# Reordering the first head pair and moving two PSUM uses in a fused hash-attention and adapter kernel

## The chip, the cores and the metric

The kernel runs on one core of a Trainium2 chip. Five engines work side by side, each through its own list of instructions: TensorE (PE, matrix products and transposes), VectorE (DVE), ScalarE (ACT), GpSimd (POOL) and SyncE (SP, here only the issue of DMAs). They meet at semaphores. The metric is the device time of one execution in microseconds (us), the median of several runs; lower is better.

## The reference

The first half is attention in which a query sees only the keys of its own hash bucket; the second sends each row of the result, heads side by side, through two of eight low-rank adapters.

```python
# q, k, v: (B, H, S, D) = (4, 8, 768, 64) float32; proj: (64, 6)
q_bucket = sum over 6 bits of (q @ proj > 0) * 2**bit      # k_bucket likewise
mask   = q_bucket[:, :, :, None] == k_bucket[:, :, None, :]
scores = where(mask, q @ k.T / sqrt(D), -1e9)
attn   = exp(scores - max) / (sum + 1e-9)
x      = (attn @ v), heads side by side                    # (3072, 512)
logits = x @ w_gate                                        # 8 experts
w      = softmax over the top 2 of logits
out    = x + sum over the 2 experts e of w_e * (x @ A[e]) @ B[e]   # A: 512x16, B: 16x512
```

## The kernel before

**Tiling.** The 32 heads are taken as 16 pairs (`p` = 0 to 15), four pairs to a batch. A pair has 2 x 768 x 768 scores, transposed (keys on partitions, queries along the row): nine tiles of 128x1024 (`s` = 0 to 8). For each, `score(p, s)` issues the matmuls (line 323) and one exponential on ScalarE (line 325) from PSUM to the bf16 tile `P`. The mask costs no pass of its own: the bf16 operand `aug[p % 2]` has 71 rows, 64 of q or k, six of signs (plus or minus 0.5, one per hash bit) and one constant, so that a score of two different buckets is pushed below what the exponential can hold. The uniform term (`uniform`, line 359: a matmul of a tiny constant with the sum of v, then a copy on VectorE) gives rows without a partner their mean.

**One pair's preparation.** `trans(p, g)`, g = 0, 1, 2, turns four 128x128 blocks of q and k at a time on TensorE (line 238) and evicts them to `qkT` (VectorE, line 245, or ScalarE). `cast` (POOL, line 276) writes 64 rows of `aug`. `hash(p)` multiplies `qkT` by the six projections (four matmuls, line 258), thresholds them to signs on VectorE (`sgn`, line 261), and SP moves the signs into `aug` by small DMAs (`sign_dma`, line 164), two in `hash`, two in `hash_b`. `vcast` (POOL) turns v to bf16 and sums it. `pvmm(p, h, i0, i1)` multiplies P by v for row blocks i0 to i1 - 1 of head h, six matmuls each (line 330); `norm` divides by the sums on VectorE (lines 374 to 379) and casts to bf16 on POOL (385).

**The adapters.** `xturn` (a transposing DMA) or, for the last pair of a batch, `xtrans` (six PE transposes into `xtp`, line 458, and a copy to `xT` on VectorE, line 460) turn x. The row blocks ("slots") of the batch before are then worked off by `moe_slot` beside the attention of later pairs: `lgz` (gate and A product, line 475), `route` (top two), `zmtrans` (line 529), `delta` (line 543). `moe_group(p)` gives two slots to pairs 5, 6, 9 and 10, one to 7, 8, 11 and 12, three to 13 and 14, and none to pairs 0 to 4.

**What sets the order.** The order is written out by hand (`tc.manual_schedule()`): `run` calls `score(p, s)`, then `first_pair(s)` for pair 0 or `pair(p, s)` for pairs 1 to 14, and `moe_slot(p, s)`; `last_pair` writes out pair 15. Every engine does its part in that order. So does SP's queue: a DMA that must wait for data holds up all DMAs that SP issues after it. PSUM has four pools: `ps_s` with two buffers of 128x1024 (score tiles), `ps_t` with one bank ("t"), `ps_v` with two ("v", the results of `pvmm`) and `ps_m` with one ("m"). A use of a bank waits until the use before it in the program has been read out.

**The first pair.** In `prologue` head 0 of pair 0 gets its own short way: `turn0` transposes it, `signs0` (line 134) computes its signs with `pst`, straight into `aug` by one threshold on VectorE for the queries and one for the keys (line 142). Head 1's signs come from `hash0(1, ...)` behind score tile 0 of pair 0: two matmuls into `hsf` (line 151) with the packed projection `proj2` (copied on VectorE, line 101), the threshold `sgnf` (line 154) and two DMAs from SP. Half of score tile 4, the first that reaches head 1, waits for those DMAs. In `first_pair` the loads of q and k of pair 2 are issued ahead of `hash0`, those of v of pairs 1 and 2 behind it:

```python
        if s == 0:
            self.load_qk(2)
            self.hash0(1, (self.nc.sync, self.nc.sync))
            self.load_v(1)
            self.load_v(2)
        if s < 3:
            self.trans(1, s, bank=None if s == 1 else (self.ps_m, "m"))
```

Of the kernel before, what the change touches and what calls it, by code (L numbers as in the profile page):

```python
# [12 lines left out]
F32 = mybir.dt.float32  # L13
# [6 lines left out]
class Emitter:  # L20
# [46 lines left out]
    def prologue(self):  # L67
        nc, sg, P, T, D, S = self.nc, self.singles, self.P, self.T, self.D, self.S

        self.pst = sg.tile([P, 6], F32, name="pst")  # L70
        nc.scalar.dma_start(out=self.pst, in_=self.proj.unsqueeze(0).to_broadcast([2, D, 6]))
        nat = self.natp.tile([P, 2, 2, T * D], F32, tag="nat", name="nat0")
        self.nat[0] = nat
        for h in range(2):
            for i, src in enumerate((self.q, self.k)):
                nc.sync.dma_start(out=nat[:, i, h], in_=src[0, h].rearrange("(p t) d -> p (t d)", t=T))
        self.load_qk(1)
        self.load_v(0)

        self.eps = sg.tile([P, P], BF16, name="eps")  # L80
        nc.vector.memset(self.eps, 2.0 ** -56)
        self.ident = sg.tile([P, P], F32, name="ident")
        make_identity(nc, self.ident)
        first = sg.tile([P, 1], F32, name="first")
        nc.scalar.activation(out=first, in_=self.eps[:, 0:1], func=ACT.Exp)
        self.proj2 = sg.tile([P, 32], F32, name="proj2")
        nc.vector.memset(self.proj2, 0.0)

        self.aug = [sg.tile([P, 4, S], BF16, name=f"aug{i}") for i in range(2)]
        for j in range(8):  # L90
            eng = nc.vector if j < 2 else nc.gpsimd
            eng.memset(self.aug[j // 4][64:96, j % 4, :], (1.0, -1.5)[j % 2])
        self.qkT[0] = self.qktp.tile([P, 2 * S], F32, tag="qkT", name="qkT0")
        self.warm(19)
        self.turn0(0, self.ps_s, "s")
        self.half0(0, 0, nc.scalar.copy)
        self.half0(0, 1, nc.scalar.copy)
        self.signs0()
        self.turn0(1, self.ps_v, "v")
        for e in range(2):  # L100
            nc.vector.tensor_copy(out=self.proj2[64 * e:64 * e + 64, e:12:2],
                                  in_=self.pst[64 * e:64 * e + 64, :])
        self.half0(1, 0, nc.gpsimd.tensor_copy)
        self.half0(1, 1, nc.gpsimd.tensor_copy)

        self.vb = []
        for i in range(3):
            a = sg.tile([P, 2, T + 1, D + 1], BF16, name=f"vb{i}")
            nc.gpsimd.memset(a[:, :, 0:T, D:D + 1], 1.0)
            nc.gpsimd.memset(a[:, :, T:T + 1, D:D + 1], float(T))  # L110
            self.vb.append(a)
        self.vcast(0)
        self.ident_bf = sg.tile([P, P], BF16, name="ident_bf")
        nc.gpsimd.tensor_copy(out=self.ident_bf, in_=self.ident)
        self.wa = sg.tile([P, self.nD, self.LZ], BF16, name="wa")
        self.Bcat = sg.tile([self.ER, self.Dm], BF16, name="Bcat")
        self.warm(6)
# [14 lines left out]


    def signs0(self):
        nc, P = self.nc, self.P
        for i in range(2):
            hs = self.ps_s.tile([P, 2, 512], F32, tag="s", name=f"hsd{i}")
            for e in range(2):
                nc.tensor.matmul(out=hs[64:70, e, 0:384], lhsT=self.pst[64 * e:64 * e + 64, :],
                                 rhs=self.qkT[0][64 * e:64 * e + 64, i * 384:(i + 1) * 384],  # L140
                                 start=True, stop=True)
            nc.vector.tensor_scalar(out=self.aug[0][64:70, i, :].rearrange("p (e c) -> p e c", e=2),
                                    in0=hs[64:70, :, 0:384], scalar1=0.0, scalar2=0.5,
                                    op0=ALU.is_gt, op1=ALU.subtract)

    def hash0(self, h, engs):
        nc = self.nc
        hs = self.ps_t.tile([self.P, 384], F32, tag="t", name=f"hsf{h}")
        rows = slice(64 * h, 64 * h + 64)
        for i in (2 * h, 2 * h + 1):  # L150
            nc.tensor.matmul(out=hs[32 * i:32 * i + 32, :], lhsT=self.proj2,
                             rhs=self.qkT[0][:, i * 384:(i + 1) * 384], start=True, stop=True)
        sgn = self.sgp.tile([self.P, 384], BF16, tag="sgn", name=f"sgnf{h}")
        nc.vector.tensor_scalar(out=sgn[rows], in0=hs[rows], scalar1=0.0, scalar2=0.5,
                                op0=ALU.is_gt, op1=ALU.subtract)
        for i in range(2):
            self.sign_dma(engs[i], 0, 2 * h + i, sgn)

    def half0(self, h, e, copy):
        copy(out=self.aug[0][0:64, 2 * h:2 * h + 2, e * 384:(e + 1) * 384],  # L160
# [190 lines left out]
        return p >= self.n_pairs - self.PPB  # L351


    def uniform(self, p):
        if self.uni_pe(p):
            return
        n = self.D + 1
        ps = self.ps_t.tile([self.P, 2, n], F32, tag="t", name=f"un{p}")
        self.nc.tensor.matmul(out=ps, lhsT=self.eps, rhs=self.vb[p % 3][:, :, self.T, :], start=True, stop=True)  # L359
        self.uni[p] = self.smallp.tile([self.P, 2, n], F32, tag="uni", name=f"uni{p}")  # L360
        self.nc.vector.tensor_copy(out=self.uni[p], in_=ps)  # L361
# [171 lines left out]
        self.acc[b, slots] = self.accp.tile([P, 3, self.Dm], F32, tag="acc", name=f"acc{b}_{slots[0]}")  # L533


    def delta(self, b, slots, i, by_pool=False, eng=None, parts=1):
        nc, P, S = self.nc, self.P, self.S
        acc, last = self.acc[b, slots], b == self.B - 1
        rows = self.out[b * S:(b + 1) * S, :].rearrange("(p t) f -> p t f", t=self.T)
        n = self.Dm // parts  # L540
        ps = (self.ps_s if last else self.ps_m).tile(
            [P, self.Dm], F32, tag="s" if last else "m", name=f"dl{b}_{slots[i]}")
        nc.tensor.matmul(out=ps, lhsT=self.zmT[b, slots][:, i * P:(i + 1) * P], rhs=self.Bcat,  # L543
                         start=True, stop=True)
        for c in [slice(j * n, (j + 1) * n) for j in range(parts)]:
            if by_pool:
                tmp = self.xp.tile([P, self.Dm], F32, tag="tmp", name=f"tmp{b}_{slots[i]}")
                nc.scalar.activation(out=tmp, in_=ps, func=ACT.Copy, scale=self.rt[b, slots][:, i:i + 1])  # L548
                nc.gpsimd.tensor_add(out=acc[:, i, :], in0=tmp, in1=self.x[b][:, slots[i], :])  # L549
            else:  # L550
                nc.vector.scalar_tensor_tensor(out=acc[:, i, c], in0=ps[:, c], scalar=self.rt[b, slots][:, i:i + 1],  # L551
                                               in1=self.x[b][:, slots[i], c], op0=ALU.mult, op1=ALU.add)
            if last:
                (eng or nc.sync).dma_start(out=rows[:, slots[i], c], in_=acc[:, i, c])
        if not last and i == len(slots) - 1:
            nc.sync.dma_start(out=rows[:, slots[0]:slots[0] + len(slots), :], in_=acc[:, 0:len(slots), :])
# [42 lines left out]
        self.last_pair(N - 1, self.B - 1)  # L599

    def first_pair(self, s):
        if s == 0:
            self.load_qk(2)
            self.hash0(1, (self.nc.sync, self.nc.sync))
            self.load_v(1)
            self.load_v(2)
        if s < 3:
            self.trans(1, s, bank=None if s == 1 else (self.ps_m, "m"))
        if s == 3:
            self.cast(1, 0)  # L610
            self.cast(1, 1)
        if s == 4:
            self.hash(1)
            self.hash_b(1)
            self.uniform(0)
        if s == 5:
            self.vcast(1)
            self.load(3)
        if s == 6:
# [1 line left out]
            self.trans(2, 0)  # L621
        if s == 7:
            self.pvmm(0, 0, 2, 4)
            self.trans(2, 1, bank=(self.ps_m, "m"))
        if s == 8:
            self.pvmm(0, 0, 4, 6)
            self.load_moe(0)
            self.load_moe(1)

    def pair(self, p, s):  # L630
        if s == 0:
            self.norm(p - 1, 0)
            self.trans(p + 1, 2)
            self.load_qk(p + 3, (0,))
        if s == 1:
            self.pvmm(p - 1, 1, 0, 2)
            self.cast(p + 1, 0)
            self.cast(p + 1, 1)
        if s == 2:
# [1 line left out]
            if p + 1 == self.n_pairs - 1:  # L641
                self.hash_b(p + 1)
            self.load_qk(p + 3, (1,))
        if s == 3:
            self.pvmm(p - 1, 1, 2, 4)
        if s == 4:
            self.pvmm(p - 1, 1, 4, 6)
            self.uniform(p)
            if p + 1 < self.n_pairs - 1:
                self.hash_b(p + 1)  # L650
        if s == 5:
            self.norm(p - 1, 1)
            self.vcast(p + 1)
            self.trans(p + 2, 0, on_act=len(self.moe_group(p)[1]) > 1)
            if p < 4:
                self.load_moe(p + 1)
            if p == 3:
# [8 lines left out]
        if s == 8:  # L666
            self.pvmm(p, 0, 3, 6)
            if p % self.PPB == 0:
                self.xtrans(p - 1)
            self.load_v(p + 3)  # L670

    def last_pair(self, p, b):
# [102 lines left out]
```

## Time and profile before

| | |
|---|---|
| median of five runs | 176.09 us |
| the five runs | 175.36, 175.99, 178.79, 176.09, 177.24 us |
| the profiled execution | 175.36 us |
| its span (first to last instruction) | 173.6 us |
| TensorE clock granted, mean | 0.984 of full speed |
| TensorE busy | 161.1 us, 93% of the span |
| ScalarE busy | 150.8 us, 87% |
| VectorE busy | 116.1 us, 67% |
| POOL busy | 115.5 us, 67% |
| the 144 exponentials, mean of one | 1029 ns |
| first score tile of pair 0 on TensorE | 7.65 us after the start of the span |
| first score tile of pair 1 | 18.75 us |

Lines of the profile name the line of the kernel, the engine, the operation, what it writes and reads (`P<-s`: the tile P from s), the shape and the count. "Idle before" is the time for which the engine had stood still just before, with the event that ended it. The chain of work that ended last is followed back from the last instruction, at each step to what released it; it shows which engine held up the end at which time. Loads of q, k and v are 384 KB each, a transfer of signs 9 KB.

### The profile page before, as it was taken

How to read it: one execution, taken by the hardware profiler on the slowest of the kernel's cores; microseconds unless marked ns; L12 is line 12 of the kernel's file. 1: busy time of each engine (PE TensorE's matmuls, PEld its weight loads, DVE VectorE, ACT ScalarE, POOL GpSimd, SP SyncE). 2: the span in 40 equal slices, each digit the busy share in tenths (PEclk: the TensorE clock that was granted, in tenths of full speed). 3: DMA queues.
4: the chain of work that ended last, by engine and by line, in shares of the span. 5: the costliest groups of instructions: out<-in, count | busy, mean ns of one | idle time of the engine just before them, and what ended most of it. 6: DMA issues, size and time to landing. Idle time of an engine off the chain costs nothing.

```text
span 173.6 us, 5249 instructions
## 1 busy us (share of the span) xinstructions
PE 161.1 (93%) x2100; PEld 111.9 (64%) x2105; DVE 116.1 (67%) x312; ACT 150.8 (87%) x176; POOL 115.5 (67%) x140
## 2 busy tenths in 40 slices
PE   7888999999999999999999999999999999998850
PEld 6355667676766676767677676767676676687610
DVE  3762666565656787878687786868785676647870
ACT  3776999999998899999997999999997988997760
POOL 8399969696988667576755676676766466630280
PEclk9999999999999999999999999999999999999985
DMA  5955497879998067697877179686954024250036
GB/s 146 301 198 185 156 254 154 162 149 190 148 220 252 27 130 225 192 187 262 137 231 228 46 136 312 131 248 196 196 169 152 9 49 183 44 197 4 2 126 237
DMA packets 30438, 28.51 MB, mean 164 GB/s; under 512 B 15078, under 2 KB 28494, under 8 KB 30414
## 3 DMA queue, kind: packets, MB, share of 16 engines
q1 hardware_dynamic: 25020, 27.38, 57.3%
q0 software_dynamic: 4832, 0.27, 4.6%
q10 hardware_dynamic: 562, 0.53, 0.9%
q8 instruction: 16, 0.26, 0.6%
q14 instruction: 8, 0.07, 0.1%
HBM read 19.42 MB, written 6.29 MB: 148 GB/s over the span
## 4 chain that ended last, share of the span: by engine, by line
PE 81%; DVE 7%; POOL 3%; issue 3%; DMA 1%; ACT 1%; SPq 1%; DVEq 0%; POOLq 0%; ACTq 0%
PE s L323 33%; PE pv L330 18%; PE tr L238 12%; PE hs L258 7%; PE lz L475 4%; PE dl L543 2%; PE warm L184 1%; PE xtp L458 1%; DVE xT L460 1%; DMA aug<-sgnf 1%; POOL xb L385 1%; POOL aug L160 1%; PE ztp L529 1%; DVE acc L551 1%; DVE qkT L131 1%
## 5 line engine op out<-in xcount | busy, mean ns | idle before, releaser
L325 ACT ACTIVATE P<-s 128x1024 bf16<-128x1024 f32 x144 | 139.7, 1029 | 11.3 <-PE s L323 9.5
L323 PE MATMUL s<-aug 71*128 71x256 bf16 (+2 forms) x408 | 86.2, 316 | 1.3 <-ACT P L325 0.6
L276 POOL CAST aug<-qkT 64x1536 bf16<-64x1536 f32 x30 | 43.9, 1463 | 12.7 <-DVE qkT L245 10.1
L330 PEld LDWEIGHTS <-P 128*128 128x128 bf16 x1080 | 44.9, 98 | 11.3
L330 PE MATMUL pv<-vb,P 128*128 128x65 bf16 x1080 | 47.5, 193 | 0.2
L323 PEld LDWEIGHTS <-aug 71*128 71x128 bf16 x408 | 32.8, 97 | 19.2 <-issue 9.9
L245 DVE TENSOR_SCALAR qkT<-tr 128x512 f32<-128x512 f32 x40 | 27.4, 685 | 8.8 <-PE tr L238 8.3
L385 POOL CAST xb<-x 128x768 bf16<-128x768 f32 x15 | 12.4, 824 | 26.2 <-DVE x L379 23.9
L238 PE MATMUL tr<-ident,nat 128*128 128x128 f32 x180 | 28.3, 279 | 0.6 <-DVE xT L460 0.6
L238 PEld LDWEIGHTS tr<-ident,nat 128*128 128x128 f32 x180 | 20.2, 140 | 10.0 <-DVE qkT L245 3.1
L261 DVE TENSOR_SCALAR sgn<-hs 128x384 bf16<-128x384 f32 x15 | 8.4, 558 | 14.5 <-PE hs L258 13.0
L379 DVE TENSOR_TENSOR x<-pv,ri 128x384 f32<-128x384 f32 x30 | 16.7, 557 | 1.0
L551 DVE SCALAR_TENSOR_TENSOR acc<-dl,rt,x 128x512 f32<-128x512 f32 (+1 forms) x21 | 15.0, 719 | 3.1 <-PE dl L543 3.1
L221 POOL TENSOR_TENSOR vs<-vn 128x384 f32<-128x384 f32 x16 | 15.9, 996 | 0.0
L374 DVE TENSOR_TENSOR pv<-pv,uni 128x390 f32<-128x390 f32 x24 | 13.6, 567 | 2.5 <-PE pv L330 2.4
L219 POOL CAST vb<-vn 128x768 bf16<-128x768 f32 x16 | 13.2, 827 | 0.3 <-DMA vn<-in_v_dram 0.2
L258 PE MATMUL hs<-qkT,proj 128*32 128x384 f32 x120 | 12.8, 498 | 0.0
L549 POOL TENSOR_TENSOR acc<-tmp,x 128x512 f32<-128x512 f32 x4 | 5.0, 1263 | 8.8 <-ACT tmp L548 8.8
L475 PE MATMUL lz<-wa,xT 128*128 128x136 bf16 x96 | 9.3, 223 | 0.6 <-ACT xT L460 0.6
L543 PE MATMUL dl<-Bcat,zmT 128*128 128x512 bf16 x19 | 7.4, 391 | 1.1 <-ACT zmT L532 0.8
L361 DVE COPY uni<-un 128x130 f32<-128x130 f32 x12 | 3.5, 294 | 7.1 <-PE un L359 7.1
L224 POOL TENSOR_TENSOR vb<-vs,vs 128x128 bf16<-128x128 f32 x16 | 7.3, 457 | 1.3
(73 smaller groups left out, 121.0 us busy)
## 6 DMA issues: line engine op xcount, KB each, us to landing
vn<-in_v_dram SPq DMA_DIRECT2D x16, 384.0 KB
nat<-in_q_dram SPq DMA_DIRECT2D x15, 384.0 KB
nat<-in_k_dram SPq DMA_DIRECT2D x15, 384.0 KB
out_dram<-acc SPq DMA_DIRECT2D x4, 512.0 KB
out_dram<-acc SPq DMA_DIRECT2D x8, 256.0 KB
out_dram<-acc SPq DMA_DIRECT2D x2, 768.0 KB
aug<-sgn SPq DMA_DIRECT2D x60, 9.0 KB
nat<-in_q_dram SPq DMA_DIRECT2D x2, 192.0 KB
```

The lines of the kernel that those rows point to most:

```text
L221: nc.gpsimd.tensor_add(out=s3, in0=vn[:, :, 0:3, :], in1=vn[:, :, 3:6, :])
L238: nc.tensor.transpose(out=ps[:, j * P:(j + 1) * P], in_=self.nat[p][:, idx % 2, idx // 2, u * P:(u + 1) * P], identity=self.ident)
L245: nc.vector.tensor_scalar(out=out, in0=ps, scalar1=2.0 ** -5, scalar2=None, op0=ALU.mult)
L258: nc.tensor.matmul(out=ps[32 * j:32 * j + 32, :], lhsT=self.proj2, rhs=self.qkT[p][:, j * 384:(j + 1) * 384], start=True, stop=True)
L276: self.nc.gpsimd.tensor_copy(out=self.aug[p % 2][0:64, :, e * n:(e + 1) * n], in_=self.qkT[p][64 * e:64 * e + 64, :].rearrange("p (j c) -> ...
L323: nc.tensor.matmul(out=ps[:, o:o + n], lhsT=aug[0:71, 2 * h + 1, kt * P:(kt + 1) * P], rhs=q, start=True, stop=True)
L325: nc.scalar.activation(out=self.P_[p][:, s * 1024:(s + 1) * 1024], in_=ps, func=ACT.Exp, scale=128.0)
L330: self.nc.tensor.matmul(out=pv, lhsT=self.p_at(p, h, kt, i), rhs=self.vb[p % 3][:, h, self.slot(kt), :], start=(start and kt == 0), stop=( ...
L379: nc.vector.tensor_tensor(out=self.x[b][:, :, c:c + D].rearrange("p (u e) d -> p e u d", e=2), in0=pv[:, 0:T, 0:D].rearrange("p (e u) d -> ...
L385: nc.gpsimd.tensor_copy(out=self.xb[b][:, hp], in_=self.x[b][:, :, hp * P:(hp + 1) * P])
L475: nc.tensor.matmul(out=lz[:, i, :], lhsT=self.xT[b][:, t, s * P:(s + 1) * P], rhs=self.wa[:, t, :], start=(t == 0), stop=(t == self.nD - 1))
L551: nc.vector.scalar_tensor_tensor(out=acc[:, i, c], in0=ps[:, c], scalar=self.rt[b, slots][:, i:i + 1], in1=self.x[b][:, slots[i], c], op0= ...
```

## The change

The edits, by place:

- Prologue: the two copies into `proj2` stand ahead of the sign thresholds of head 0. The threshold for the keys becomes two instructions of 6x384 instead of one of 6x768; `signs0` is divided into helpers (`hash0`, `sign0`), and the old `hash0` becomes `hash1(p, h)` with the same instructions.
- Pair 0, SP's queue: the two sign transfers of head 1 are issued ahead of the loads of q and k of pair 2, with v of pairs 1 and 2 behind those.
- Pair 0, TensorE: the three transpose groups of pair 1 stand behind score tiles 1, 2 and 3 instead of 0, 1 and 2. They keep their banks.
- Pair 0: the uniform term stands behind tile 5 instead of tile 4, and in bank m instead of bank t.
- Pairs 5, 6, 9 and 10: `pvmm` of head 1 of the pair before takes row blocks 0; 1, 2; 3, 4; 5 behind tiles 1, 3, 4 and 5, instead of 0, 1; 2, 3; 4, 5 behind tiles 1, 3 and 4. Other pairs keep theirs.
- Pairs 4, 8 and 12, tile 8: `xtrans` of the pair before uses bank m instead of bank t.
- `delta` takes a bank as an argument, which no caller gives.

```diff
@@ -95,11 +95,11 @@
         self.turn0(0, self.ps_s, "s")
         self.half0(0, 0, nc.scalar.copy)
         self.half0(0, 1, nc.scalar.copy)
-        self.signs0()
-        self.turn0(1, self.ps_v, "v")
         for e in range(2):
             nc.vector.tensor_copy(out=self.proj2[64 * e:64 * e + 64, e:12:2],
                                   in_=self.pst[64 * e:64 * e + 64, :])
+        self.signs0()
+        self.turn0(1, self.ps_v, "v")
         self.half0(1, 0, nc.gpsimd.tensor_copy)
         self.half0(1, 1, nc.gpsimd.tensor_copy)
 
@@ -132,29 +132,39 @@
 
 
     def signs0(self):
-        nc, P = self.nc, self.P
         for i in range(2):
-            hs = self.ps_s.tile([P, 2, 512], F32, tag="s", name=f"hsd{i}")
+            hs = self.ps_s.tile([self.P, 2, 512], F32, tag="s", name=f"hsd{i}")
             for e in range(2):
-                nc.tensor.matmul(out=hs[64:70, e, 0:384], lhsT=self.pst[64 * e:64 * e + 64, :],
-                                 rhs=self.qkT[0][64 * e:64 * e + 64, i * 384:(i + 1) * 384],
-                                 start=True, stop=True)
-            nc.vector.tensor_scalar(out=self.aug[0][64:70, i, :].rearrange("p (e c) -> p e c", e=2),
-                                    in0=hs[64:70, :, 0:384], scalar1=0.0, scalar2=0.5,
-                                    op0=ALU.is_gt, op1=ALU.subtract)
-
-    def hash0(self, h, engs):
+                self.hash0(i, e, hs[:, e, 0:384])
+            if i == 0:
+                self.sign0(i, hs[:, :, 0:384], 0, 2)
+            else:
+                for e in range(2):
+                    self.sign0(i, hs[:, e:e + 1, 0:384], e, e + 1)
+
+    def hash0(self, j, e, out):
+        self.nc.tensor.matmul(out=out[64:70], lhsT=self.pst[64 * e:64 * e + 64, :],
+                              rhs=self.qkT[0][64 * e:64 * e + 64, j * 384:(j + 1) * 384],
+                              start=True, stop=True)
+
+    def sign0(self, j, hs, e0, e1):
+        self.nc.vector.tensor_scalar(
+            out=self.aug[0][64:70, j, e0 * 384:e1 * 384].rearrange("p (e c) -> p e c", c=384),
+            in0=hs[64:70], scalar1=0.0, scalar2=0.5, op0=ALU.is_gt, op1=ALU.subtract)
+
+
+    def hash1(self, p, h):
         nc = self.nc
-        hs = self.ps_t.tile([self.P, 384], F32, tag="t", name=f"hsf{h}")
+        hs = self.ps_t.tile([self.P, 384], F32, tag="t", name=f"hsf{p}_{h}")
         rows = slice(64 * h, 64 * h + 64)
-        for i in (2 * h, 2 * h + 1):
-            nc.tensor.matmul(out=hs[32 * i:32 * i + 32, :], lhsT=self.proj2,
-                             rhs=self.qkT[0][:, i * 384:(i + 1) * 384], start=True, stop=True)
-        sgn = self.sgp.tile([self.P, 384], BF16, tag="sgn", name=f"sgnf{h}")
+        for j in (2 * h, 2 * h + 1):
+            nc.tensor.matmul(out=hs[32 * j:32 * j + 32, :], lhsT=self.proj2,
+                             rhs=self.qkT[p][:, j * 384:(j + 1) * 384], start=True, stop=True)
+        sgn = self.sgp.tile([self.P, 384], BF16, tag="sgn", name=f"sgnf{p}_{h}")
         nc.vector.tensor_scalar(out=sgn[rows], in0=hs[rows], scalar1=0.0, scalar2=0.5,
                                 op0=ALU.is_gt, op1=ALU.subtract)
-        for i in range(2):
-            self.sign_dma(engs[i], 0, 2 * h + i, sgn)
+        for j in (2 * h, 2 * h + 1):
+            self.sign_dma(nc.sync, p, j, sgn)
 
     def half0(self, h, e, copy):
         copy(out=self.aug[0][0:64, 2 * h:2 * h + 2, e * 384:(e + 1) * 384],
@@ -351,11 +361,12 @@
         return p >= self.n_pairs - self.PPB
 
 
-    def uniform(self, p):
+    def uniform(self, p, bank=None):
         if self.uni_pe(p):
             return
         n = self.D + 1
-        ps = self.ps_t.tile([self.P, 2, n], F32, tag="t", name=f"un{p}")
+        pool, tag = bank or (self.ps_t, "t")
+        ps = pool.tile([self.P, 2, n], F32, tag=tag, name=f"un{p}")
         self.nc.tensor.matmul(out=ps, lhsT=self.eps, rhs=self.vb[p % 3][:, :, self.T, :], start=True, stop=True)
         self.uni[p] = self.smallp.tile([self.P, 2, n], F32, tag="uni", name=f"uni{p}")
         self.nc.vector.tensor_copy(out=self.uni[p], in_=ps)
@@ -533,13 +544,13 @@
         self.acc[b, slots] = self.accp.tile([P, 3, self.Dm], F32, tag="acc", name=f"acc{b}_{slots[0]}")
 
 
-    def delta(self, b, slots, i, by_pool=False, eng=None, parts=1):
+    def delta(self, b, slots, i, by_pool=False, eng=None, parts=1, bank=None):
         nc, P, S = self.nc, self.P, self.S
         acc, last = self.acc[b, slots], b == self.B - 1
         rows = self.out[b * S:(b + 1) * S, :].rearrange("(p t) f -> p t f", t=self.T)
         n = self.Dm // parts
-        ps = (self.ps_s if last else self.ps_m).tile(
-            [P, self.Dm], F32, tag="s" if last else "m", name=f"dl{b}_{slots[i]}")
+        pool, tag = bank or ((self.ps_s, "s") if last else (self.ps_m, "m"))
+        ps = pool.tile([P, self.Dm], F32, tag=tag, name=f"dl{b}_{slots[i]}")
         nc.tensor.matmul(out=ps, lhsT=self.zmT[b, slots][:, i * P:(i + 1) * P], rhs=self.Bcat,
                          start=True, stop=True)
         for c in [slice(j * n, (j + 1) * n) for j in range(parts)]:
@@ -599,21 +610,22 @@
         self.last_pair(N - 1, self.B - 1)
 
     def first_pair(self, s):
+        M = (self.ps_m, "m")
         if s == 0:
+            self.hash1(0, 1)
             self.load_qk(2)
-            self.hash0(1, (self.nc.sync, self.nc.sync))
             self.load_v(1)
             self.load_v(2)
-        if s < 3:
-            self.trans(1, s, bank=None if s == 1 else (self.ps_m, "m"))
+        if 0 < s < 4:
+            self.trans(1, s - 1, bank=M if s != 2 else None)
         if s == 3:
             self.cast(1, 0)
             self.cast(1, 1)
         if s == 4:
             self.hash(1)
             self.hash_b(1)
-            self.uniform(0)
         if s == 5:
+            self.uniform(0, bank=M)
             self.vcast(1)
             self.load(3)
         if s == 6:
@@ -621,19 +633,23 @@
             self.trans(2, 0)
         if s == 7:
             self.pvmm(0, 0, 2, 4)
-            self.trans(2, 1, bank=(self.ps_m, "m"))
+            self.trans(2, 1, bank=M)
         if s == 8:
             self.pvmm(0, 0, 4, 6)
             self.load_moe(0)
             self.load_moe(1)
 
     def pair(self, p, s):
+        n = len(self.moe_group(p)[1])
+
+        for at, i0, i1 in ((1, 0, 1), (3, 1, 3), (4, 3, 5), (5, 5, 6)) if n == 2 else ((1, 0, 2), (3, 2, 4), (4, 4, 6)):
+            if s == at:
+                self.pvmm(p - 1, 1, i0, i1)
         if s == 0:
             self.norm(p - 1, 0)
             self.trans(p + 1, 2)
             self.load_qk(p + 3, (0,))
         if s == 1:
-            self.pvmm(p - 1, 1, 0, 2)
             self.cast(p + 1, 0)
             self.cast(p + 1, 1)
         if s == 2:
@@ -641,17 +657,14 @@
             if p + 1 == self.n_pairs - 1:
                 self.hash_b(p + 1)
             self.load_qk(p + 3, (1,))
-        if s == 3:
-            self.pvmm(p - 1, 1, 2, 4)
         if s == 4:
-            self.pvmm(p - 1, 1, 4, 6)
             self.uniform(p)
             if p + 1 < self.n_pairs - 1:
                 self.hash_b(p + 1)
         if s == 5:
             self.norm(p - 1, 1)
             self.vcast(p + 1)
-            self.trans(p + 2, 0, on_act=len(self.moe_group(p)[1]) > 1)
+            self.trans(p + 2, 0, on_act=n > 1)
             if p < 4:
                 self.load_moe(p + 1)
             if p == 3:
@@ -666,7 +679,7 @@
         if s == 8:
             self.pvmm(p, 0, 3, 6)
             if p % self.PPB == 0:
-                self.xtrans(p - 1)
+                self.xtrans(p - 1, bank=(self.ps_m, "m"))
             self.load_v(p + 3)
 
     def last_pair(self, p, b):
```

## The prediction

> **What bounds the kernel now.** I read the page's busy shares first, then its chain of work that ended last, then the row of the exponentials.
>
> ```profile
> PE 161.1 (93%) x2100; PEld 111.9 (64%) x2105; DVE 116.1 (67%) x312; ACT 150.8 (87%) x176; POOL 115.5 (67%) x140
> PE 81%; DVE 7%; POOL 3%; issue 3%; DMA 1%; ACT 1%; SPq 1%; DVEq 0%; POOLq 0%; ACTq 0%
> L325 ACT ACTIVATE P<-s 128x1024 bf16<-128x1024 f32 x144 | 139.7, 1029 | 11.3 <-PE s L323 9.5
> ```
>
> TensorE carries 81% of the chain; ScalarE waits 9.5 us for score matmuls, never long the other way. So time is won only where TensorE itself stands still, or does less. The change removes no matmul, so I looked for TensorE's idle stretches. In the chain, opened in order of time, the start has one:
>
> ```profile
> 9.99 0.96 SPq L164
> 11.06 1.91 DMA aug<-sgnf
> 13.43 0.83 PE hs L258 x8
> 14.28 0.57 DVE sgn L261
> 15.13 0.87 PE s L323 x6
> ```
>
> Here the chain leaves TensorE twice: for the sign transfers of pair 0's second head, and for the threshold `sgn` on VectorE. The timeline of that stretch prices both (in brackets the idle time before, and who ended it):
>
> ```profile
> 13.06 0.38 PE L323 MATMUL s<-aug 71*128 71x512 bf16 x1 [0.36 <-DMA aug<-sgnf]
> 14.28 0.56 DVE L261 TENSOR_SCALAR sgn<-hs 128x384 bf16<-128x384 f32 x1 [1.94 <-PE hs L258]
> 14.90 0.23 PE L359 MATMUL un<-vb,eps 128*128 128x130 bf16 x1 [0.68 <-DVE sgn L261]
> 15.60 1.94 ACT L325 ACTIVATE P<-s 128x1024 bf16<-128x1024 f32 x2 [1.11 <-PE s L323]
> ```
>
> The other stretch that the change touches recurs where pair 5, 9 and 13 begin:
>
> ```profile
> 54.29 0.49 PE L458 MATMUL xtp<-ident_bf,xb 128*128 128x128 bf16 x6
> 54.62 0.60 PE L323 MATMUL s<-aug 71*128 71x512 bf16 x3
> 54.82 0.56 DVE L460 COPY xT<-xtp 128x768 bf16<-128x768 bf16 x1 [0.81 <-PE xtp L458]
> 55.44 0.66 PE L238 MATMUL tr<-ident,nat 128*128 128x128 f32 x4 [0.21 <-DVE xT L460]
> 56.80 1.02 ACT L325 ACTIVATE P<-s 128x1024 bf16<-128x1024 f32 x1 [0.46 <-PE s L323]
> ```
>
> The transposes `tr` need the one "t" bank, which holds `xtp` until VectorE has copied it out. Score tile 0 is issued by 55.05 and `tr` starts at 55.44: TensorE stands 0.39 us (0.387 from the single records), three times.
>
> **Start, what TensorE gains.** The proj2 copies (8.05 to 8.38, waited for by `hsf`) move ahead of the first threshold. That lets `hsf` start 0.16 us sooner, its threshold end about 9.75 (was 9.91), and SP issue the sign transfers at about 9.8 (was 9.99). The split threshold costs VectorE about 0.08 us (two of about 0.48, an estimate, for one of 0.95), yet score tile 0 needs only its first half: 7.29, just behind the last warming matmul, for 7.65. Moving the transposes of pair 1 behind tile 1 brings tile 1 forward by about a microsecond (they waited for a load that landed at 9.25), but that is worth nothing by itself, since half of tile 4 still waits for the signs. Those land 0.2 to 0.45 us sooner: 0.2 from the earlier issue; the rest if the second transfer no longer runs beside queued loads.
>
> `un` leaves the place behind `hs`. Its wait of 0.75 us (matmul `hs` issued through at 14.15, `un` at 14.90) goes, for `un` in bank m behind tile 5 finds its bank free: the eviction of pair 1's last transposes is due about 12.4. So tiles 5 and 6 come 0.95 to 1.2 us sooner. Were this all, pair 1 would begin that much sooner.
>
> **Start, what SP's queue gives back.** SP takes its commands in order, and the two sign transfers wait for VectorE.
>
> ```profile
> 4.13 0.47 SPq L201 DMA_DIRECT2D nat<-in_q_dram  x1
> 4.64 0.92 SPq L201 DMA_DIRECT2D nat<-in_k_dram  x1
> 9.99 1.79 SPq L164 DMA_DIRECT2D aug<-sgnf  x2
> 11.84 0.94 SPq L210 DMA_DIRECT2D vn<-in_v_dram  x2
> 14.90 3.50 SPq L164 DMA_DIRECT2D aug<-sgn  x4
> ```
>
> Pair 2's q and k loads stand behind them now: issued at about 11.5 instead of 4.1 and 4.6. Queued loads land 1.03 us apart (single records: 8.22, 9.25, 10.30, 11.34, 12.35), and one issued to a quiet ring took 3.37 us (vn1, 11.84 to 15.2). So q lands about 14.9, k 15.9, vn1 16.9, vn2 17.9 (before: 11.34, 12.35, 15.2, 16.2). Two things wait for this. The fourth transpose of pair 2's first group needs k; it would be ready about 15.5, so TensorE stands 0.4 us, and the nominal gain falls to 0.55–0.8. And pair 1's four sign transfers, issued at about 14.5, stand behind all four loads.
>
> [...] **Start: +0.3 us**, where TensorE's own order gave −0.65.
>
> What is hidden: pair 1's values are cast later by 0.3 to 1.1 us on POOL, which idles between (67% busy); the next user is the cast for pair 2, due about 28. [...]
>
> **The transposed x in bank m.** `tr` finds bank t free and follows tile 0 directly. `lz` in bank m now waits for the copy `xT`, which it reads anyway: no new wait. After it VectorE still has the sum, reciprocal and product before it evicts `tr` at 56.60, so the matmul that next needs that eviction (`hs`, done waiting at 57.34, started at 57.74) has 0.40 us of cover, about what is won. Gain 0.387 each: at pair 13 all of it.
>
> **Finer pieces, pairs 5, 6, 9, 10.** Six matmuls of head 1 (0.177 us of TensorE) move from behind tile 1 to behind tile 5. No work is saved. Pairs 5 and 9: `hs` would then be reached 0.387+0.177 = 0.564 us sooner, against a cover of 0.40, so 0.165 is lost to a new wait for VectorE's eviction; but later tiles of these pairs regain 0.10 (in tile 8 TensorE waits for ScalarE by that much; with tiles spaced more evenly it need not). Net −0.31 with the bank. Pairs 6 and 10: −0.10 each, by that wait alone; bounds 0 and −0.15. VectorE's norm of head 1 waits for the late piece, about 0.9 us later than now; behind it stand only the transfer of x by way of POOL, which idles 23.9 us for it in all. Sum: −0.387 −2×0.31 −2×0.10 = **−1.2 us** (bounds −0.8 and −1.4).
>
> The bank argument of `delta` and the divided helpers issue the same instructions: nothing.
>
> **Sum.** +0.3 −1.2 = −0.9 us. TensorE carries the chain from there to the tail, so it arrives whole. The profiled execution, 175.36 (span 173.6 and 1.76 around it), becomes 174.5; it was the fastest of the five shown and lies 0.73 below their median. Median: 176.09 −0.9 = **175.2 us**.
>
> **The rivals.**
> - *Rings not late* (0.23). A sign transfer is in after 1.91 us; were the first load, on a quiet ring, as fast and not 3.37, all four would be in by about 16.5, and the signs on free rings. Then −0.65 −1.2 = −1.85: 174.2 (173.8 to 174.6). [...]
> - *The boundaries don't pay* (0.12): VectorE sets `hs` in pairs 5, 9, 13, and the pieces only move waits. Left is about −0.3 with the start's +0.3: 176.1. For it: VectorE's copy, sum, product and eviction follow one another from 54.82 to 57.28, so the eviction hardly moves. Against: the 0.40 us by which `hs` started after it could.
> - *Slower* (0.15): pair 1's signs come after both the loads and a fetch on the same engine, the loads themselves starting late: 17.9 + 1.0 (one more load's turn) + 1.2 (fetch) = 20.1 or later. It decides from 20.0, where the start's +1.2 eats the −1.2; at 20.5 the start costs 1.6, so +0.4: 176.5, and past 21.9 it would be over 1% slower.
> - *Likeliest, as summed* (0.50): 174.7 to 175.9.
>
> **How the numbers follow.** About 1%, 1.76 us, is what a measurement of this kernel can tell from no change: the borders are 174.33 and 177.85. Below lie three fifths of the first rival and a sixth of the likeliest case, 0.14 + 0.08 = 0.22. Above lies the slower rival's far part and what I have not thought of, 0.09. Within: 0.69. The range leaves out one in ten on each side: from within the first rival, 173.9, to just past the slower rival's price, 176.7.
>
> **What would show it.** In the changed profile: tile 5 of pair 0 at about 13.9 (14.97), with no wait of `un` for `sgn`; pair 2's k load landing near 15.9 and a wait of `tr` for it; the first tile of pair 1 waiting for `aug<-sgn` and starting at 18.8 to 19.45; no wait `tr` for `xT` in the list of waits (3 times, 1.5 us in the weight loads before); at pair 5, `hs` behind a short wait for `qkT`. The prediction is wrong if pair 1 starts before 18.5 or after 20.0, or if the stretch from pair 1 to the end is not about 1.2 us shorter.

## The result and the profile after

The changed kernel took 174.35 us in the median of 43 runs, the kernel before 176.31 in 80. The ratio is 0.990, with a 95% interval of 0.9885 to 0.9915: −1.76 us (−2.0 to −1.5). A second set, taken with the experiments, gave 174.98 against 176.27, ratio 0.9937 (0.9912 to 0.9963): −1.1 us (−1.55 to −0.65). The two intervals just meet. The forecast was 175.2, a ratio of 0.995, within the range of 173.9 to 176.7. Direction and size hold by the second set; by the first the gain is twice the forecast of −0.9 us.

In some executions TensorE's granted clock falls to half for some microseconds in pair 0 (0.51 between 15.20 and 22.10 us in the profile of the pieces alone), and the comparisons leave out most of these (all that took over 1.5% more than the fastest), but not all.

The page of the changed kernel, the same three lines:

```profile
PE 161.6 (93%) x2100; PEld 112.2 (65%) x2105; DVE 116.9 (67%) x313; ACT 150.9 (87%) x176; POOL 115.5 (67%) x140
PE 76%; DVE 9%; POOL 6%; issue 3%; DMA 2%; ACT 1%; SPq 0%; DVEq 0%; POOLq 0%; ACTq 0%
L335 ACT ACTIVATE P<-s 128x1024 bf16<-128x1024 f32 x144 | 139.8, 1027 | 10.0 <-PE s L333 8.4
```

Its span is 173.6 us, that of before to the tenth. This execution took 175.41 us, about 1 us above its kernel's median, and its start came late: TensorE's granted clock, half at first, rose to full at 7.30 us, in before's profile at 4.05 (equal matmuls `warm` start 0.107 us apart ahead of the rise and 0.055 behind it, in both). The matmuls of the first signs, in before a group of 1.46 us, show it:

```profile
4.88 2.64 PE L146 MATMUL hsd<-qkT,pst 64*6 64x384 f32 x8
```

So the two profiles must not be subtracted end from end. What can be compared is each stretch, from a fixed event in it. From pair 1's first exponential to the end of the span it is 154.09 us before and 152.76 after: −1.33, for a forecast of about −1.2. The pair-0 stretch of after, in the timeline:

```profile
13.87 0.38 PE L333 MATMUL s<-aug 71*128 71x512 bf16 x1 [0.85 <-DMA aug<-sgnf]
15.40 0.22 PE L370 MATMUL un<-vb,eps 128*128 128x130 bf16 x1
15.60 1.94 ACT L335 ACTIVATE P<-s 128x1024 bf16<-128x1024 f32 x2 [0.30 <-PE s L333]
16.95 0.33 PE L248 MATMUL tr<-ident,nat 128*128 128x128 f32 x1 [0.15 <-DMA nat<-in_k_dram]
20.25 0.59 PE L333 MATMUL s<-aug 71*128 71x512 bf16 x3 [0.90 <-DMA aug<-sgn]
20.88 1.94 ACT L335 ACTIVATE P<-s 128x1024 bf16<-128x1024 f32 x2 [0.84 <-PE s L333]
```

`un` waits for nothing now, and ScalarE's pause before tile 5 is 0.30 us, where it was 1.11. But two new waits are there: a transpose for pair 2's k, and, the larger, pair 1's first tile for its signs. SP's queue shows which loads now stand ahead of them (pair 2's q goes out at 12.63, behind the sign transfers, where before it went out at 4.13, ahead of them):

```profile
10.79 1.79 SPq L174 DMA_DIRECT2D aug<-sgnf  x2
12.63 0.43 SPq L211 DMA_DIRECT2D nat<-in_q_dram  x1
13.12 0.45 SPq L211 DMA_DIRECT2D nat<-in_k_dram  x1
13.62 0.98 SPq L220 DMA_DIRECT2D vn<-in_v_dram  x2
15.72 3.22 SPq L174 DMA_DIRECT2D aug<-sgn  x4
```

And the start of pair 5, where `tr` now begins before VectorE has finished `xT`:

```profile
55.63 0.50 PE L469 MATMUL xtp<-ident_bf,xb 128*128 128x128 bf16 x6
55.97 0.60 PE L333 MATMUL s<-aug 71*128 71x512 bf16 x3
56.17 0.56 DVE L471 COPY xT<-xtp 128x768 bf16<-128x768 bf16 x1 [0.81 <-PE xtp L469]
56.40 0.60 PE L248 MATMUL tr<-ident,nat 128*128 128x128 f32 x4
56.66 2.99 ACT L335 ACTIVATE P<-s 128x1024 bf16<-128x1024 f32 x3 [0.35 <-PE s L333]
```

ScalarE runs three exponentials with hardly a pause, where before it stood 0.46 us after the first. From the last exponential of pair 4 to the first of pair 14 the timeline gives 88.61 us before and 87.31 after: −1.30.

### The profile page after: what moved, and what is told of

Same layout as the page of the kernel before. It is cut to its first block, busy times and chain, and to the rows that moved or that the text cites. A ratio compares the mean times of both kernels' runs of the same rounds, so it can differ in the third digit from the quotient of the medians.

```text
span 173.6 us, 5251 instructions
## 1 busy us (share of the span) xinstructions
PE 161.6 (93%) x2100; PEld 112.2 (65%) x2105; DVE 116.9 (67%) x313; ACT 150.9 (87%) x176; POOL 115.5 (67%) x140
## 4 chain that ended last, share of the span: by engine, by line
PE 76%; DVE 9%; POOL 6%; issue 3%; DMA 2%; ACT 1%; SPq 0%; DVEq 0%; POOLq 0%; ACTq 0%
PE s L333 30%; PE pv L340 17%; PE tr L248 11%; PE hs L268 6%; PE lz L486 3%; DMA aug<-sgn 2%; PE dl L554 2%; PE hsd L146 2%; PE warm L194 1%; PE xtp L469 1%; POOL vs L231 1%; DVE qkT L255 1%; DVE acc L562 1%; DVE x L390 1%; POOL xb L396 1%
## 5 line engine op out<-in xcount | busy, mean ns | idle before, releaser
L340 PEld LDWEIGHTS <-P 128*128 128x128 bf16 x1080 | 45.4, 98 | 11.8
L340 PE MATMUL pv<-vb,P 128*128 128x65 bf16 x1080 | 48.1, 193 | 0.2
```

The costliest lines, as they stand in the source:

```text
L340: self.nc.tensor.matmul(out=pv, lhsT=self.p_at(p, h, kt, i), rhs=self.vb[p % 3][:, h, self.slot(kt), :], start=(start and kt == 0), stop=( ...
```

## The experiments

**Each part alone.** Three kernels take one part of the change each.

The bank alone:

```diff
-                self.xtrans(p - 1)
+                self.xtrans(p - 1, bank=(self.ps_m, "m"))
```

> The kernel before with one edit: xtrans of pairs 3, 7 and 11 writes bank m instead of bank t. My prediction's step: TensorE no longer stands before the transposes at pairs 5, 9 and 13, 0.387 us each, so -1.16 us against before. The trace of after moved by -0.43 at each of the three places (pieces included at two of them); if the bank alone does that, -1.3 us. Rival (VectorE's eviction sets hs behind it): the gain is given back within the pair, -0.3 us or less.

The finer pieces alone: `pair` as in the change, all else as before.

> The kernel before with one edit: the finer pieces of pvmm in pairs 5, 6, 9 and 10. My prediction's step: without the bank edit TensorE reaches hs 0.177 us sooner and VectorE's eviction still has 0.40 us of cover, so nothing is lost, and tile 8's wait for ScalarE goes: 0.10 us for each of four pairs, -0.4 us in all. Rival from the trace of after (pairs 5 and 6 together won as much as pair 13, where only the bank changed): the pieces are worth nothing, 0 +- 0.1 us.

The start alone:

```diff
-        for at, i0, i1 in ((1, 0, 1), (3, 1, 3), (4, 3, 5), (5, 5, 6)) if n == 2 else ((1, 0, 2), (3, 2, 4), (4, 4, 6)):
+        for at, i0, i1 in ((1, 0, 2), (3, 2, 4), (4, 4, 6)):
...
-                self.xtrans(p - 1, bank=(self.ps_m, "m"))
+                self.xtrans(p - 1)
```

> The changed kernel without its finer pieces and with xtrans back in bank t: only prologue, first pair and SP's order differ from before. By my prediction +0.3 us against before (pair 1's signs late behind the loads; bounds -0.05 to +0.7). By the rival that the measured total of after (-1.76 by the ratio) leaves once 1.3 us of it lie at the boundaries: -0.46 us (-0.2 to -0.7), the first tile of pair 1 starting at about 18.2 in a run whose TensorE clock rises as early as in the profile of before.

Measured against before: bank alone 0.9938 (0.9906 to 0.9969), −1.1 us; pieces alone 0.9973 (0.9946 to 1.0000), −0.5; start alone 1.0008 (0.9980 to 1.0036), +0.1. The falls of the clock blur these ratios: the kernel before has one in 22 of its 46 runs here, the start alone in 1 of 14. In the runs without a fall (mean granted clock of 0.977 or more) before took 176.00 us in the mean, the bank alone 174.97, the pieces alone 175.70 and the start alone 176.25: −1.0, −0.3 and +0.25 (about −0.1 to +0.6). The traces are sharper, since behind pair 4 the executions agree to 0.02 us. From the last exponential of pair 4 (us):

| | to pair 8's last | pair 8's to pair 12's | to pair 14's first | sum against before |
|---|---|---|---|---|
| before | 38.12 | 38.07 | 12.42 | |
| bank alone | 37.72 | 37.67 | 11.99 | −1.23 |
| pieces alone | 37.90 | 37.85 | 12.43 | −0.43 |
| start alone | 38.13 | 38.07 | 12.41 | 0.00 |
| the change | 37.69 | 37.63 | 11.99 | −1.30 |

The parts do not add: −1.23 and −0.43 would be −1.66. With both, 0.18 us is lost in each of the pairs 5 and 9. From first exponential to first exponential, pair 5 of after gives back 0.08 of what the bank alone won, and pair 6 wins 0.11. Where TensorE reaches `hs` sooner, it stands before it, until VectorE has evicted `qkT`. Before, these waits were 1.3 us in all, 4 of them, the longest 0.3; the list of waits of after has:

```profile
PEld hs L268 <- DVE qkT L255: 2.0, 5, 0.5
```

**The queue.** Is it the loads that make pair 1's signs late? First the change with pair 2's q and k ahead of the sign transfers again:

```diff
-            self.hash1(0, 1)
             self.load_qk(2)
+            self.hash1(0, 1)
```

> The changed kernel with one edit: SP issues pair 2's loads of q and k ahead of the sign transfers of head 1 again, as before. If the queue order costs what my prediction says, this is faster than the changed kernel by 0.7 to 0.95 us (start -0.65 instead of +0.3), so about -2.6 against before. If the loads do not delay pair 1's signs, it is no faster: equal within 0.2 us, or slower by up to 0.3 since the signs of head 1 land later.

Ratio 0.9886 (0.9833 to 0.9938), −2.0 us. The expected −2.6 did not come, and this interval does not part it from the changed kernel; the trace does. I count from SP's first command for head 1's signs to pair 1's first exponential, which leaves most of the clock's rise out. In the old order: command at 9.83, exponential at 18.60, and no pause from tile 8 on (four exponentials in one piece):

```profile
17.68 3.77 ACT L335 ACTIVATE P<-s 128x1024 bf16<-128x1024 f32 x4 [0.18 <-PE s L333]
```

That is 8.77 us, for 10.09 in the changed kernel (10.79 to 20.88) and 9.51 in before (9.99 to 19.50). A second profile of the changed kernel shows how far this varies:

> The changed kernel once more, for a second look at its start. In its first profile TensorE's clock rose only at 7.3 us (4.05 in the profile of before), and pair 1's first exponential began at 20.9. If the start costs 0.3 us by itself, a profile with a rise before 5 us shows that exponential at about 19.8 (before: 19.50), waiting for the signs; if the start gains as the total of the runs suggests (-0.46), at about 19.0. Time against before: -1.3 to -1.8 us.

```profile
10.28 1.79 SPq L174 DMA_DIRECT2D aug<-sgnf  x2
16.49 0.33 PE L248 MATMUL tr<-ident,nat 128*128 128x128 f32 x1 [0.21 <-DMA nat<-in_k_dram]
19.52 0.59 PE L333 MATMUL s<-aug 71*128 71x512 bf16 x3 [0.63 <-DMA aug<-sgn]
20.15 1.02 ACT L335 ACTIVATE P<-s 128x1024 bf16<-128x1024 f32 x1 [0.56 <-PE s L333]
```

9.87 us here; in the start alone, whose pair 0 is the same, 9.49:

```profile
19.21 0.59 PE L333 MATMUL s<-aug 71*128 71x512 bf16 x3 [0.17 <-DMA aug<-sgn]
```

So by pair 1's first exponential the new order costs 0.7, 1.1 and 1.3 us in three profiles. Part of it comes back a pair later: from there to pair 2's first exponential the old order takes 9.29 us, the new one 8.86, so that 0.3, 0.7 and 0.9 us are left. And it buys nothing: from SP's command to the half of tile 4 that waits for head 1's signs it is 3.05 to 3.08 us in all twelve profiles, in either order.

In the single records of the second profile, the first two of pair 1's sign transfers had five of six shares in by 18.70 and 18.87, behind the loads (pair 2's v: most shares by 18.5), and the last at 19.24 and 19.43. In the old order, where pair 2's v was in by 16.19, all their shares were in by 16.73 and 17.52. A 16 KB instruction fetch ran from 16.50 to 17.60. That it held the last shares up is not shown: the records name no DMA engine, and in the old order a fetch from 15.60 to 16.63 made no share late. In the start alone the fetch began at 15.88 and the signs were in by 18.93 and 19.12.

The same from the other side, before with the sign transfers first:

```diff
-            self.load_qk(2)
             self.hash0(1, (self.nc.sync, self.nc.sync))
+            self.load_qk(2)
```

> The kernel before with one edit: SP issues the sign transfers of head 1 ahead of pair 2's loads of q and k. By my prediction's step the four loads now lie ahead of pair 1's signs, whose first tile starts at 18.9 to 19.6 instead of 18.75: +0.2 to +0.8 us against before. Rival (the rings are not the limit): 0 +- 0.15.

Ratio 1.0044 (1.0017 to 1.0071): +0.8 us; +0.7 in the runs without a fall. Its profile has a fallen clock from 16.00 to 19.41 us, so no place is read from it.

Then one load fewer ahead of pair 1's signs, in the changed kernel:

```diff
             self.load_v(1)
-            self.load_v(2)
...
             self.vcast(1)
+            self.load_v(2)
             self.load(3)
```

> The changed kernel with one edit: the load of v of pair 2 is issued behind pair 1's four sign transfers. One load less lies ahead of them. By the ring step of my prediction they land 1.03 us sooner, the first tile of pair 1 no longer waits for them (0.63 us in the second profile of the changed kernel), and the time falls by 0.4 to 0.7 us against the changed kernel. Rival (the signs are late for another reason, say SP's own pace): no change, 0 +- 0.15.

Pair 1's first tile waits no more; the stretch is 9.13 us (9.84 to 18.97), and the transpose's wait for k remains. But the gain is given back in the next pair:

```profile
18.05 2.85 ACT L335 ACTIVATE P<-s 128x1024 bf16<-128x1024 f32 x3 [0.25 <-PE s L333]
25.09 0.33 PE L248 MATMUL tr<-ident,nat 128*128 128x128 f32 x1 [0.53 <-DMA nat<-in_k_dram]
25.89 1.02 ACT L335 ACTIVATE P<-s 128x1024 bf16<-128x1024 f32 x1 [1.04 <-PE s L333]
```

The load of v that was put behind now delays pair 3's k, and ScalarE stands 1.04 us in pair 1. The time, ratio 0.9891 (0.9841 to 0.9941), cannot be told from the changed kernel's. That the loads ahead delay the signs is shown; the expected saving is not.

**The uniform term alone.**

```diff
             self.hash_b(1)
-            self.uniform(0)
         if s == 5:
+            self.uniform(0, bank=(self.ps_m, "m"))
```

> The kernel before with one edit: the uniform term of pair 0 stands behind tile 5 and in bank m. TensorE's wait of 0.75 us before tile 5 goes. [...] Clock theory: TensorE's idle stretch between 13 and 15 us makes the clock fall in part of the runs of before (granted clock 0.968 to 0.973 in 22 of 46); without the stretch this share sinks to a fifth or less.

Ratio 0.9966 (0.9939 to 0.9992), −0.6 us; −0.4 in the runs without a fall. Its stretch is 8.88 us (10.26 to 19.14) for 9.51. In this profile pair 2's start gave 0.6 us of that back (first exponential at 28.64, 9.50 after pair 1's, for 8.90 before): SP's loads are no sooner, and pair 2's first tile waits for its signs behind them:

```profile
27.95 0.59 PE L323 MATMUL s<-aug 71*128 71x512 bf16 x3 [0.47 <-DMA aug<-sgn]
```

Of 22 runs none had a mean granted clock below 0.977; of the runs of before beside it, 23 of 57.

**The clock.** Does the pause before `un` let the clock fall? The kernel before, with useless matmuls put into the pause:

```diff
             self.hash_b(1)
+            self.warm(8)
             self.uniform(0)
```

> The kernel before with eight useless 128x128 matmuls (0.083 us each) behind hs of pair 1, in the stretch of 0.75 us in which TensorE waits for VectorE's threshold. They save nothing. Clock theory: the pause is what lets the granted clock fall to half in part of the runs of before (mean granted clock below 0.977 in 22 of 46 and 23 of 57 runs); filled, this happens in a fifth of the runs or less, and the runs without a fall take as long as before's (176.0), within 0.2. Rival (the fall has nothing to do with the pause): four runs in ten as before.

None of 22 runs fell below 0.977; before beside it, 9 of 27. Ratio 0.9982 (0.9963 to 1.0002). The runs without a fall took 175.90 in the mean, before's 175.96. Eight matmuls that compute nothing cost nothing that these runs show, and keep the clock up:

```profile
14.49 0.62 PE L184 MATMUL warm<-eps 128*128 128x128 bf16 x8
15.24 0.23 PE L359 MATMUL un<-vb,eps 128*128 128x130 bf16 x1
```

**A better version.** The change with the old order of loads and signs, with finer pieces in pairs 6 and 10 only, and with one load less ahead of pair 2's signs (in the old-order run ScalarE had stood 0.46 us at pair 2's start):

```diff
-            self.hash1(0, 1)
             self.load_qk(2)
+            self.hash1(0, 1)
...
-... ((1, 0, 1), (3, 1, 3), (4, 3, 5), (5, 5, 6)) if n == 2 else ...
+... ((1, 0, 1), (3, 1, 3), (4, 3, 5), (5, 5, 6)) if p in (6, 10) else ...
...
-            self.load_qk(p + 3, (0,))
+            if p != 1:
+                self.load_qk(p + 3, (0,))
...
-            self.load_qk(p + 3, (1,))
+            self.load_qk(p + 3, (0, 1) if p == 1 else (1,))
```

> The changed kernel with three edits: pair 2's loads of q and k ahead of the sign transfers again; in pair 1 the load of q of pair 4 behind the first two sign transfers of pair 2 (in the run with the old queue order these landed late and cost 0.39 us at pair 2); finer pieces in pairs 6 and 10 only (with bank m they cost 0.07 us in pairs 5 and 9). Expected against the changed kernel: 0.4 to 0.8 from the queue, 0.4 from pair 2's signs, 0.14 from the pieces, together -0.9 to -1.3 us; if the signs of pair 2 wait for something else, -0.5 to -0.9.

173.08 us, ratio 0.9846 (0.9804 to 0.9888), −2.7 us; its six runs lie between 172.85 and 173.82, and the fastest run of the changed kernel took 173.64.

```profile
9.69 1.79 SPq L174 DMA_DIRECT2D aug<-sgnf  x2
17.53 3.77 ACT L335 ACTIVATE P<-s 128x1024 bf16<-128x1024 f32 x4 [0.18 <-PE s L333]
```

8.76 us from the command to pair 1's first exponential (18.45), pair 2's first 8.86 after it, and 87.17 us from pair 4 to pair 14: all three edits arrive. Against the second profile of the changed kernel that is −1.11 and −0.13, within the −0.9 to −1.3 expected; the runs without a fall differ by −1.6, of which the rest has not been placed.

## Why the prediction was right, and where its size was off

*The bank.* Forecast 0.387 us at each of three places; the bank alone gave 0.40, 0.40 and 0.43. Right; the rival "the boundaries don't pay" is refuted.

*The pieces.* Forecast with the bank: pair 5 at −0.31, pair 6 at −0.10, the loss at `hs` being the eviction's cover of 0.40 us overdrawn. The trace of after: −0.33 and −0.10, and the wait for `qkT` has grown as said (0.18 us lost by the parts' sum, 0.165 forecast). Alone, with the cover in place, they give 0.21 us for two pairs. Right; the sum of this part was −1.2, measured −1.30.

*`un`.* Forecast 0.75 us of TensorE's time. The stretch with no late load shrank from 9.51 to 8.77: 0.74; `un` alone gave 0.63. Right.

*The earlier sign command.* Forecast 9.8 for 9.99. With the clock's rise between 4.3 and 4.7 us the kernels with the new prologue issue it at 9.69, 9.83 and 9.84; those with the old one at 9.99 (rise at 4.05), 10.06 (5.01) and 10.34 (4.33). Right within that scatter. In the best of these the late half of tile 4 came at 12.76 (13.06), 0.30 sooner. That lies within the 0.2 to 0.45 forecast, but it is the earlier command alone, in a kernel with the old order: the second term, a faster landing ahead of the loads, is nothing (3.07 us from the command in both). So the reordering of SP's queue brought only its cost.

*The queue.* Forecast: it takes back 0.95 us of the start's nominal gain. Measured 0.7 to 1.3, by the two waits that were named. Taken as a time of day, the forecast's own sign failed in the profile of after: pair 1's first tile began at 20.25, past 20.0, with the clock's late rise in it; in the second profile it began at 19.52. From the sign command, forecast at 9.8, the forecast start was 9.0 to 9.65 us away; measured 9.46, 9.24 and, in the start alone, 8.86. What the shares of the second profile show is signs behind loads: five of six by 18.70 and 18.87, most of pair 2's v by 18.5. That a fetch adds its 1.2 us to the landing, as in the rival "slower", no run shows: with one from 15.60 to 16.63 the old order had all shares of pair 1's first two sign transfers in by 16.73 and 17.52. The rival "rings not late" is refuted by all three profiles of this start: each has its tile waiting for the signs.

*The start's sum.* −0.15 − 0.74 + 0.7 to 1.3 lies between −0.2 and +0.4; the forecast +0.3 was in its upper part. How that +0.3 comes about, out of the late landing of the signs, was the author's estimate, and no run shows the term itself; what the runs showed in its place is the start alone, +0.1 (−0.35 to +0.6) with the falls, +0.25 without.

The steps therefore hold, and the runs without a fall bear them out: −1.30 at the boundaries and +0.25 make −1.05, and the second set without falls gave −1.1 (174.84 for 175.94), for a forecast of −0.9. The first set gave −1.76. Of its runs of before that were compared, 13 lie between 176.9 and 177.5 us, 1.3 above the others; where the clock of such a run is recorded it had fallen (15 of 16). They raise the mean of the 66 by 0.25, which leaves −1.5. What the prediction did not see at all is that `un`'s pause had this second price, the clock (below 0.977 in 23 of 57 runs of before, in none of 22 with `un` moved). The last 0.4 us between the sets lie mostly in the changed kernel, not in before: its runs without a fall took 174.5 in the first set and 174.8 in the second, those of before 176.0 and 175.9. That difference is not clear of noise (0.3 us, about 0 to 0.7); the scatter of the signs' landing, 0.6 us between three profiles, is large enough for it, but that it differed between the sets is not shown. So the sum was right in direction and mechanism, and that its size met the second set so closely is in part luck: the start's scatter alone is two thirds of it.

## What to carry to other kernels

When DMAs change places in a queue, count which transfers then stand ahead of small ones that somebody waits for, with the time at which each lands, before counting the gain: here the moved signs landed no faster (3.07 us from the command in either order), and those behind came up to 1.3 us later. Two edits that both bring an engine to the same wait share its cover, so price them together (−1.66 by the parts, −1.30 in fact). And compare two profiles stretch by stretch from a common event: here both spans are 173.6 us, and the kernels differ by more than 1 us.

## What the runs showed of the hardware that was not expected

*The clock's rise varied by over 3 us.* In the twelve profiles TensorE's clock rose between 4.05 and 7.30 us after the start. Two kernels with the same start show what it moves: the first exponential of before began at 8.28, with the rise at 4.05, that of the bank alone at 9.20, with the rise at 7.21.

*It can fall after a stretch in which TensorE was busy for 61%, with no pause over 0.75 us.* In the profile of the pieces alone, the clock rose at 5.01, fell at 15.25 and rose again at 22.07 us: 10.24 and 6.82, three and two times 3.41. The full clock of before lasted from 4.05 to 167.89 us, that of after from 7.30 to 167.73: 163.84 and 160.43, 48 and 47 times 3.413. By stretches of time (columns: busy time and count of PE, PEld, DVE, ACT, POOL; granted clock; DMA share; GB/s), first the 3.40 us ahead of that fall at 15.25, then the stretch that it slowed:

```profile
11.80:15.20 3.40, 2.08 (x16) 0.61 (x15) 1.17 (x2) 2.48 (x3) 3.18 (x6) 1.00 0.66 180
15.20:22.10 6.90, 6.90 (x56) 5.15 (x55) 1.68 (x3) 3.45 (x4) 5.59 (x7) 0.51 0.43 141
```

With the clock up, before does 88 matmuls in the second stretch, where these are 56. The kernel before has the same 2.08 us of 3.40 between 12.0 and 15.4:

```profile
12.00:15.40 3.40, 2.08 (x15) 0.62 (x14) 1.13 (x3) 2.21 (x3) 3.18 (x6) 1.00 0.70 220
```

The clock stayed up there. Counted in steps of 3.413 us from the rise at 4.05, the borders lie at 10.9, 14.3 and 17.7, so that no step had the whole of it; that this is the reason is the author's inference. With the useless matmuls it is 2.64 us:

```profile
12.00:15.40 3.40, 2.64 (x23) 1.06 (x22) 1.24 (x2) 2.56 (x3) 3.18 (x6) 1.00 0.58 179
```

The twelve profiles can be counted in the same way. Cut into steps of 3.413 us from the rise on, they have 14 falls, two of them in pair 0 and twelve where the kernel runs out. Each comes at the end of a step in which TensorE was busy for 64% or less. Of the 556 other steps at full clock one was that low (59%, at the end of the kernel with useless matmuls); all the rest had 66% or more. The two nearest to the border, with a fall at its end (before with the sign transfers first) and without one (one load fewer ahead of the signs):

```profile
12.59:16.00 3.41, 2.17 (x15) 0.71 (x15) 1.07 (x3) 2.09 (x3) 3.25 (x5) 1.00 0.74 232
161.67:165.09 3.42, 2.25 (x34) 1.57 (x32) 2.79 (x17) 2.23 (x7) 1.57 (x2) 1.00 0.00 0
```

So in these traces a fall goes with a step of low busy share, 64% or less. That the share brings it about, and that the place of the steps decides whether an execution of before falls, was the author's inference: the one profile of before has no fall in pair 0.

Counted over all the runs, a mean granted clock below 0.977 was seen in 75 of 191 runs of kernels that keep the pause (before in three sets, bank alone, pieces alone, signs first), and in 4 of 140 of those that end or fill it, the changed kernel's first set included. In the kernel before, a fall costs 1.4 us (15 runs, clock 0.971 to 0.973) or 2.6 (39 runs, below 0.97), far more than the pause of 0.75 itself.
